# Weight loads in half-transfers of even and odd rows, and a last strip in pieces of 112, 8 and 8 rows, in a decode kernel that streams 89 MB

## The chip, the cores and the metric

The kernel runs on one core of one Trainium2 chip. The time is the device time of one execution in microseconds (us); the lower the better. Before the change it takes 217.38 us, the median of three runs (217.35 to 217.49).

## The reference

Two tokens (B = 2) pass through one decode step of windowed attention, gated by a small MLP:

```python
xn = layernorm(x)                                  # x: (2, 1, 512)
q  = xn @ wq                                       # wq: (512, 4096), 32 heads of 128
k, v = k_cache[:, :, -4096:], v_cache[:, :, -4096:]  # 8 key/value heads, window of 4096
s  = softmax(q k^T / sqrt(128)) v                  # 4 query heads share a key/value head
s  = s.reshape(2, 4096) @ wo                       # wo: (4096, 512)
z  = gelu(xn @ w_in)                               # w_in: (512, 1792)
g  = silu((z1 * (w_sp * layernorm(z2) + b_sp)) @ w_out)   # w_out: (896, 512)
out = x + s * g
```

All of it is in 32-bit floats. Nearly all of the 89.4 MB that are read are the two windows of the caches (32 MiB each) and the weights: w_q 8 MiB, w_o 8 MiB, w_in 3.5 MiB, w_out 1.75 MiB. Each byte is used for two tokens only.

## The kernel before

All large loads go to one ring of four buffers ("slot"), 128 rows of 32 KB each. In order: the two halves of w_q (`wq0`, `wq1`, 32 KB a row), `win` (28 KB a row), `wout` (14 KB a row), then the keys and values of eight units (`k0`, `k1`, `v0`, `k2`, `v1`, ... `v7`, 32 KB a row; a unit is two heads of one token), and last w_o in seven pieces of 8, 8, 8, 4, 2, 1 and 1 blocks of 2 KB a row. A load into a buffer that is still read waits for its readers.

All of these are issued by SP (SyncE), one instruction for each transfer, in the order of the program (the class `InOrder` keeps each engine's instructions in the order in which the code stands; it records every instruction under line 37, so the profile's rows all say L37, and tiles are told by name). ACT (ScalarE) issues three tiny loads at the start: `xs` (two rows of 2 KB) and the two numbers of `wb`. `x`, eight rows of 512 B, is loaded behind the second piece of w_o. A transfer is cut into packets, one for each row here, which 16 DMA engines work off; at the end of its share each of them writes one packet of 4 bytes that counts towards the transfer's completion (the trace has 16 of them for such a transfer). Each transfer has one of eight such counters, named DMAHW0 to DMAHW7 in the lists below; a transfer that takes a counter again waits until the earlier transfer on it is complete.

On the engines: TensorE (PE) makes q from w_q as 128 rows of `wq0` and `wq1` land, then z from `win` and y from `wout`. For a unit VectorE (DVE) transposes the keys in four parts (`kt`), PE makes shares of the scores (`sh`), ACT copies them (`shs`), PE adds them (`s`); then come the maximum, the exponentials (`p`), their transpose (`pT`) and the sum over the values (`acc`). The last w_o blocks go into `part` and `so`; the tail after the last w_o piece is eight small matmuls, two VectorE instructions (`res`) and the store of the output.

Of the kernel before, what the change touches and what calls it, by code (L numbers as in the profile page):

```python
# [14 lines left out]
P = 128  # L15
# [27 lines left out]
def kernel(  # L43
# [14 lines left out]
    pe, dve, act, sp = (InOrder(tc, e) for e in (nc.tensor, nc.vector, nc.scalar, nc.sync))  # L58
# [22 lines left out]
    def slot(name):  # L81
        return ring.tile([P, SLOT], F32, tag="slot", name=name)
# [5 lines left out]
        return ps.tile([P, 512], F32, tag=tag, name=name, bufs=BANKS[tag])  # L88


    xs = cst.tile([B, D], F32, tag="xs", name="xs")
    act.dma_start(xs, x[:, 0, :])
    wq_v = wq.rearrange("(p k) f -> p k f", p=P)
    wqt = []
    for a in range(2):
        t = slot(f"wq{a}")
        sp.dma_start(t, wq_v[:, 2 * a : 2 * a + 2, :].rearrange("p k f -> p (k f)"))
        wqt.append(t.rearrange("p (k f) -> p k f", k=2))
    win = slot("win")[:, : KT * F]
    sp.dma_start(win, w_in.rearrange("(p k) f -> p (k f)", p=P))  # L100
    win = win.rearrange("p (k f) -> p k f", k=KT)
    wout = slot("wout")[:, : FT * D]
    sp.dma_start(wout, w_out.rearrange("(p j) d -> p (j d)", p=P))
    wout = wout.rearrange("p (j d) -> p j d", j=FT)

    wb1 = cst.tile([1, 2], F32, tag="wb1", name="wb1")
# [3 lines left out]
    def by_group(t):  # L110

        return bass.AP(tensor=t.tensor, offset=t.offset, ap=[[DC, G], [D, B], [1, DC]])
# [309 lines left out]
    wo_v = wo.rearrange("(p j) d -> p j d", j=32)  # L422
    blocks = []
    pieces = ((8, 8), (8,), (4, 2, 1, 1))
    j = 0
    for i, piece in enumerate(pieces):
        t = slot(f"wo{i}").rearrange("p (j d) -> p j d", d=D)
        at = 0
        for n in piece:
            sp.dma_start(t[:, at : at + n, :], wo_v[:, j : j + n, :])  # L430
            blocks += [(t, at + a) for a in range(n)]
            at, j = at + n, j + n
            if j == 16:
                sp.dma_start(x4[0:P:16, :], by_group(x))
# [47 lines left out]
    for n in range(EARLY):  # L482
        t, a = blocks[n]
# [5 lines left out]
    for n in range(EARLY, 32):  # L489
        if n == LATE:  # L490
            spread_quarters(so, parts, start=False, stop=False)
        t, a = blocks[n]
# [37 lines left out]
```

## Time and profile before

| what | value | how to read it |
|---|---|---|
| median of three runs | 217.38 us | the time that the change is measured against |
| the profiled execution | 217.5 us, span 215.7 us | the span runs from the first to the last instruction; 1.8 us lie around it |
| PE, DVE, ACT busy | 72%, 50%, 20% of the span | shares of busy time |
| loads on SP's queue (q1) | 96.8% of 16 DMA engines' span | time in packets |
| bytes read from HBM | 89.40 MB, 414 GB/s over the span | |
| instruction loads (q8) and table loads (q14) | 7 packets and 2 | they use the same 16 DMA engines |
| the chain that ended last | DMA 44%, PE 31%, DVE 19% | steps followed back from the last instruction |

A view of the DMA can be asked for a stretch of the span. It counts the packets that *start* in the stretch, their bytes, and their whole time as a share of 16 engines over the stretch. In a short stretch that share can therefore be over 100%, since packets run on past its end; share times length times 16, over the number of packets, is the mean time of a packet.

### The profile page before, as it was taken

How to read it: one execution, taken by the hardware profiler on the slowest of the kernel's cores; microseconds unless marked ns; L12 is line 12 of the kernel's file. 1: busy time of each engine (PE TensorE's matmuls, PEld its weight loads, DVE VectorE, ACT ScalarE, POOL GpSimd, SP SyncE). 2: the span in 40 equal slices, each digit the busy share in tenths (PEclk: the TensorE clock that was granted, in tenths of full speed). 3: DMA queues.
4: the chain of work that ended last, by engine and by line, in shares of the span. 5: the costliest groups of instructions: out<-in, count | busy, mean ns of one | idle time of the engine just before them, and what ended most of it. 6: DMA issues, size and time to landing. Idle time of an engine off the chain costs nothing.

```text
span 215.7 us, 2229 instructions
## 1 busy us (share of the span) xinstructions
PE 155.7 (72%) x866; PEld 43.6 (20%) x866; DVE 108.5 (50%) x176; ACT 44.1 (20%) x109; POOL 2.6 (1%) x14
## 2 busy tenths in 40 slices
PE   0164856151796997899699599459959948998883
PEld 0110212110121222222122222222212212231311
DVE  3400072425976944963946851685577089240101
ACT  5000001401123115114303404120431421242001
POOL 4000000000000000000000000000000000000000
PEclk9999788755589699799889879958988995999699
DMA  7998999999999999999999999999999999999990
GB/s 292 389 486 389 425 433 454 451 416 431 444 395 474 395 459 413 450 425 431 437 400 456 413 444 428 431 437 431 431 407 453 419 444 431 431 401 416 425 377 35
DMA packets 3929, 89.54 MB, mean 415 GB/s; under 512 B 446, under 2 KB 462, under 8 KB 848
## 3 DMA queue, kind: packets, MB, share of 16 engines
q1 hardware_dynamic: 3912, 89.40, 96.8%
q8 instruction: 7, 0.11, 0.2%
q14 instruction: 2, 0.02, 0.0%
q10 hardware_dynamic: 8, 0.00, 0.0%
HBM read 89.40 MB, written 0.00 MB: 414 GB/s over the span
## 4 chain that ended last, share of the span: by engine, by line
DMA 44%; PE 31%; DVE 19%; issue 3%; ACT 1%; SPq 0%; DVEq 0%
DMA k<-in_A_k_cache_dram 22%; DMA win<-in_B_w_in_dram 14%; DVE kt L37 13%; PE s L37 9%; PE sh L37 9%; DMA wo<-in_A_wo_dram 8%; PE acc L37 6%; PE z L37 2%; PE y L37 2%; PE mo L37 1%; DVE gate L37 1%; PE col L37 1%; PE so L37 1%; DVE u L37 1%; DVE m L37 1%
## 5 line engine op out<-in xcount | busy, mean ns | idle before, releaser
L37 DVE STREAM_TRANSPOSE kt<-k 128x2048 f32<-128x2048 f32 x32 | 72.4, 2293 | 24.9 <-DMA k<-in_A_k_cache_dram 24.9
L37 PE MATMUL sh<-kt,qbd 128*32 128x512 f32 x256 | 41.5, 682 | 14.0 <-DVE kt L37 14.0
L37 PE MATMUL s<-shs,add_dq 128*128 128x512 f32 x64 | 41.0, 748 | 0.0
L37 ACT ACTIVATE shs<-sh 128x512 f32<-128x512 f32 x32 | 19.1, 597 | 100.9 <-PE sh L37 100.9
L37 PE MATMUL acc<-v,pT 128*32 128x512 f32 x256 | 32.0, 641 | 0.2 <-DVE pT L37 0.2
L37 PE MATMUL q_ps<-wq,xnT 128*32 128x512 f32 x64 | 11.0, 850 | 9.9 <-DMA wq<-in_A_wq_dram 9.9
L37 PEld LDWEIGHTS s<-shs,add_dq 128*128 128x128 f32 x64 | 11.2, 219 | 28.3 <-issue 23.9
L37 PEld LDWEIGHTS sh<-kt,qbd 128*32 128x32 f32 x256 | 6.9, 115 | 33.9 <-issue 19.6
L37 PEld LDWEIGHTS acc<-v,pT 128*32 128x32 f32 x256 | 7.7, 118 | 25.8 <-issue 23.0
L37 DVE TENSOR_REDUCE m<-s 128x2 f32<-128x512 f32 x8 | 5.4, 680 | 14.0 <-PE s L37 14.0
L37 PE MATMUL mo<-l,same_r 128*128 128x2 f32 x16 | 3.5, 287 | 10.7 <-ACT p L37 10.7
L37 DVE STREAM_TRANSPOSE qT<-q_ps 128x512 f32<-128x512 f32 x2 | 1.4, 717 | 18.1 <-PE q_ps L37 18.1
L37 ACT ACTIVATE o<-acc,wd 128x128 f32<-128x128 f32 x32 | 9.1, 373 | 3.4 <-PE acc L37 3.4
L37 ACT ACTIVATE p<-s,nb 128x256 f32<-128x256 f32 x16 | 7.6, 490 | 7.1 <-DVE nb L37 6.9
L37 PE MATMUL part<-wo,oT 128*32 128x512 f32 x56 | 8.2, 722 | 1.1 <-DMA wo<-in_A_wo_dram 0.8
L37 PE MATMUL col<-o,sel 128*32 128x512 f32 x16 | 8.3, 601 | 0.4 <-ACT o L37 0.4
L37 ACT ACTIVATE zs<-z 128x448 f32<-128x448 f32 x1 | 0.5, 544 | 30.9 <-PE z L37 30.9
L37 PE MATMUL y<-wout,hT 128*32 128x512 f32 x14 | 3.6, 1059 | 3.8 <-issue 3.8
L37 PEld LDWEIGHTS q_ps<-wq,xnT 128*32 128x32 f32 x64 | 2.6, 144 | 17.1 <-issue 12.2
L37 DVE STREAM_TRANSPOSE pT<-p 128x512 f32<-128x512 f32 x8 | 5.4, 675 | 1.2 <-ACT p L37 1.2
L37 DVE TENSOR_TENSOR res<-so,gate 128x128 f32<-128x128 f32 x1 | 0.3, 292 | 11.1 <-PE so L37 11.1
L37 ACT ACT_TABLE_LOAD x4 | 5.1, 1283 | 1.9 <-issue 1.9
(106 smaller groups left out, 66.8 us busy)
## 6 DMA issues: line engine op xcount, KB each, us to landing
k<-in_A_k_cache_dram SPq DMA_DIRECT2D x8, 4096.0 KB, 21.3
v<-in_A_v_cache_dram SPq DMA_DIRECT2D x8, 4096.0 KB, 26.7
wq<-in_A_wq_dram SPq DMA_DIRECT2D x2, 4096.0 KB, 21.3
wo<-in_A_wo_dram SPq DMA_DIRECT2D x3, 2048.0 KB
win<-in_B_w_in_dram SPq DMA_DIRECT2D x1, 3584.0 KB, 29.3
wout<-in_B_w_out_dram SPq DMA_DIRECT2D x1, 1792.0 KB, 33.1
wo<-in_A_wo_dram SPq DMA_DIRECT2D x1, 1024.0 KB
wo<-in_A_wo_dram SPq DMA_DIRECT2D x1, 512.0 KB, 17.4
```

The costliest lines, as they stand in the source:

```text
L37: return self.tc.keep_in_program_order(call(*args, **kwargs))
```

## The change

The kernel's loads of weights are cut otherwise; what is computed, and every instruction of PE, DVE, ACT and GpSimd, stays. `wq0`, `win`, `wout` and the first piece of w_o are each loaded in two transfers of 64 rows, the even rows and then the odd ones. Of `wq1` the first 24 KB of each row come as even and odd rows too; the last 8 KB of each row (2048 numbers) come in three transfers, of rows 0 to 111, 112 to 119 and 120 to 127. All other pieces of w_o, the keys and the values are loaded as before.

```diff
+    def even_odd(dst, src):
+        for r in range(2):
+            sp.dma_start(dst[r:P:2], src[r:P:2])
+
+    def low_heavy(dst, src, n):
+        at = src.shape[1] - n
+        even_odd(dst[:, :at], src[:, :at])
+        for rows in (slice(0, 112), slice(112, 120), slice(120, P)):
+            sp.dma_start(dst[rows, at:], src[rows, at:])
...
         t = slot(f"wq{a}")
-        sp.dma_start(t, wq_v[:, 2 * a : 2 * a + 2, :].rearrange("p k f -> p (k f)"))
+        src = wq_v[:, 2 * a : 2 * a + 2, :].rearrange("p k f -> p (k f)")
+        even_odd(t, src) if a == 0 else low_heavy(t, src, 2048)
...
-    sp.dma_start(win, w_in.rearrange("(p k) f -> p (k f)", p=P))
+    even_odd(win, w_in.rearrange("(p k) f -> p (k f)", p=P))
...
-    sp.dma_start(wout, w_out.rearrange("(p j) d -> p (j d)", p=P))
+    even_odd(wout, w_out.rearrange("(p j) d -> p (j d)", p=P))
...
-            sp.dma_start(t[:, at : at + n, :], wo_v[:, j : j + n, :])
+            if j == 0:
+                even_odd(t[:, at : at + n, :], wo_v[:, j : j + n, :])
+            else:
+                sp.dma_start(t[:, at : at + n, :], wo_v[:, j : j + n, :])
```

The start of SP's program before, from the first load of w_q to the second load of keys (a row has the tile, the source, and rows by numbers a row; `wq_69` and `wq_71` are the two halves, `k_281` and `k_283` the first two units' keys; in brackets is what the instruction waits for):

```order
L37 DMA wq_69<-in_A_wq_dram 128x8192
L37 DMA wq_71<-in_A_wq_dram 128x8192
L37 DMA win<-in_B_w_in_dram 128x7168
L37 DMA wout<-in_B_w_out_dram 128x3584
L37 DMA k_281<-in_A_k_cache_dram 128x1x8192 [waits DMAHW1_49,PE_49]
L37 DMA k_283<-in_A_k_cache_dram 128x1x8192 [waits DMAHW4_49,DMAHW0_49,PE_49]
```

The same place now (`wq_72` is the second half, `k_288` and `k_290` the keys):

```order
L37 DMA wq_69<-in_A_wq_dram 64x8192 x2
L37 DMA wq_72<-in_A_wq_dram 64x6144 x2
L37 DMA wq_72<-in_A_wq_dram 112x2048
L37 DMA wq_72<-in_A_wq_dram 8x2048 [waits DMAHW0_49]
L37 DMA wq_72<-in_A_wq_dram 8x2048 [waits DMAHW1_49]
L37 DMA win<-in_B_w_in_dram 64x7168 [waits DMAHW2_49]
L37 DMA win<-in_B_w_in_dram 64x7168 [waits DMAHW3_49]
L37 DMA wout<-in_B_w_out_dram 64x3584 [waits DMAHW4_49]
L37 DMA wout<-in_B_w_out_dram 64x3584 [waits DMAHW5_49]
L37 DMA k_288<-in_A_k_cache_dram 128x1x8192 [waits DMAHW6_49,PE_49]
L37 DMA k_290<-in_A_k_cache_dram 128x1x8192 [waits DMAHW1_49,DMAHW7_49,DMAHW0_49,PE_49]
```

Four transfers have become eleven, and six of them now wait until a counter of an earlier transfer is free.

The end of SP's program before, from the first piece of w_o to the store:

```order
L37 DMA wo_313<-in_A_wo_dram 128x4096 x2
L37 DMA x_91<-in_A_x_dram 8x1x128
L37 DMA wo_317<-in_A_wo_dram 128x4096
L37 DMA wo_319<-in_A_wo_dram 128x2048
L37 DMA wo_319<-in_A_wo_dram 128x1024
L37 DMA wo_319<-in_A_wo_dram 128x512 x2
L37 DMA out_dram<-res 4x2x128
```

The same place now:

```order
L37 DMA wo_320<-in_A_wo_dram 64x4096 x2
L37 DMA wo_320<-in_A_wo_dram 128x4096
L37 DMA x_98<-in_A_x_dram 8x1x128
L37 DMA wo_325<-in_A_wo_dram 128x4096
L37 DMA wo_327<-in_A_wo_dram 128x2048
L37 DMA wo_327<-in_A_wo_dram 128x1024
L37 DMA wo_327<-in_A_wo_dram 128x512 x2
L37 DMA out_dram<-res 4x2x128
```

Only the first piece has become two; the order is the same.

## The prediction

> **What bounds the kernel now.** I read the page first: the slices of the DMA, its queues, and the chain that ended last.
>
> ```profile
> DMA  7998999999999999999999999999999999999990
> GB/s 292 389 486 389 425 433 454 451 416 431 444 395 474 395 459 413 450 425 431 437 400 456 413 444 428 431 437 431 431 407 453 419 444 431 431 401 416 425 377 35
> q1 hardware_dynamic: 3912, 89.40, 96.8%
> DMA 44%; PE 31%; DVE 19%; issue 3%; ACT 1%; SPq 0%; DVEq 0%
> ```
>
> The DMA engines are busy from the first slice to the last but one, so the 19% of VectorE and 31% of TensorE in the chain run beside transfers. To see whether the engines ever wait for an issue, I asked for the tiles of the keys and of w_o (minimum, median and maximum from issue to landing), and for the end of the chain in order of time.
>
> ```profile
> DMA to landing us min/median/max: 19.0/21.3/23.9
> DMA to landing us min/median/max: 17.4/17.5/17.7
> 193.29 17.36 DMA wo<-in_A_wo_dram
> ...
> 210.70 1.24 PE so L37 x32
> ...
> 211.97 0.47 PE so L37 x8
> ...
> 212.46 0.30 DVE res L37
> ```
>
> A load of keys lands at the earliest 19.0 us after its issue, and its own packets are eight an engine. Next, the DMA in stretches: the middle of the kernel, 13 to 21 us (32 KB packets alone), 31.4 to 34.2 us (14 KB packets alone) and 207 to 212 us.
>
> ```profile
> DMA packets 3261, 85.92 MB, mean 430 GB/s; under 512 B 360, under 2 KB 368, under 8 KB 368
> q1 hardware_dynamic: 3249, 85.81, 99.8%
> q8 instruction: 6, 0.10, 0.2%
> q14 instruction: 2, 0.02, 0.0%
> ...
> q1 hardware_dynamic: 112, 3.67, 106.1%
> ...
> q1 hardware_dynamic: 85, 1.22, 101.5%
> ...
> GB/s 328 393 393 492 426 393 360 426 459 393 328 393 475 361 360 328 459 377 393 426 311 295 213 164 197 180 197 180 180 164 180 115 180 131 115 49 0 0 0 0
> ```
>
> From 4 to 204 us the 16 engines are full (99.8%) at 430 GB/s. A 32 KB packet takes 1.061 x 8 x 16 / 112 = 1.213 us, so a load of keys is 9.7 us of transfer, and its issue is 19.0 - 9.7 = 9.3 us ahead of need at the least. The kernel is bound by its bytes; the time can move only at the start, in the tail, or in how evenly the 16 engines finish. The last row shows that they don't finish evenly: about 209.6 us the rate falls from some 400 to 180 GB/s, half of the engines, for the last 1.7 us. I looked for the reason at one transfer's completions, the second piece of w_o, in four stretches from 199.5 to 200.05, 200.85, 201.25 and 201.6 us, and at one load of instructions (44.2 to 45.3 us).
>
> ```profile
> DMA packets 29, 0.25 MB, mean 451 GB/s; under 512 B 10, under 2 KB 14, under 8 KB 14
> DMA packets 31, 0.38 MB, mean 474 GB/s; under 512 B 4, under 2 KB 8, under 8 KB 8
> DMA packets 9, 0.15 MB, mean 369 GB/s; under 512 B 0, under 2 KB 0, under 8 KB 0
> DMA packets 19, 0.21 MB, mean 609 GB/s; under 512 B 6, under 2 KB 6, under 8 KB 6
> ...
> q8 instruction: 1, 0.02, 6.1%
> ```
>
> Packets under 512 B are completions; those from there to 2 KB are the rows of x, queued right behind. The first stretch has 4 rows of x and 10 completions (two of them x's, so 8 engines finish w_o there); the second again 4 rows of x and 4 completions (two engines); the third none; the fourth six. So eight engines are on time, two are up to 1.3 us late, and six are 1.2 to 2.1 us late. That is the count of the middle stretch: two table loads and six instruction loads, each of which takes time (6.1% of 1.1 x 16 = 1.07 us, and more for what it disturbs) from one engine. The last six set the end. x has eight rows and ran on four engines, two of them on time, the other two the pair that is mildly late; none of the six is among those four.
>
> **The change part by part.** *Shift of bytes.* The strip of 8 KB was 8 rows an engine. If 112 rows go evenly over 16 engines, that is 7 each, and if the two pieces of 8 rows go one row each to the same eight engines, those have 9 and the other eight 7. Price: a 14 KB packet takes 1.015 x 2.8 x 16 / 85 = 0.535 us; with 1.213 us for 32 KB that is 0.0376 us a KB and 0.008 us a packet, so 0.309 us for 8 KB and 0.911 us for 24 KB. Before, wq1 cost an engine 8 x 1.213 = 9.70 us. Now it costs 8 x 0.911 + 7 x 0.309 = 9.45 us, or with 9 strips 10.07: -0.25 us, or +0.37.
>
> *More completions.* Each engine gets one more for wq0, win, wout and the first piece of w_o, and two more for wq1 (four more on the eight that take the small pieces): 6 or 8. No row has one alone; their price lies between nothing and the 0.008 us of a packet. I take the upper end, 0.05 to 0.06 us. So the light engines end 0.20 us earlier and the heavy ones 0.43 us later.
>
> *Who is last.* If the six late engines are light, the fourth stretch above (201.25 to 201.6) moves to 201.05 to 201.4. The pair, if heavy, moves from at most 200.85 to at most 201.28, still not last, and the eight on time stay far ahead. Every later transfer is alike on all engines, so this order holds to the end: -0.20 us. The tail behind the last w_o piece (0.47 + 2 x 0.30 us and the store) stays.
>
> *Even and odd halves.* They move the same bytes. Their price for the rate lies between nothing and a slower rate of the 7 + 3.5 + 1.75 + 2 MiB, of which I know no row; the nearest rows are the full 430 GB/s of all other loads, so I take nothing.
>
> *The start.* Rows from 1.64 to 2.4 us, 2.4 to 2.8 us and 3.5 to 4 us, and the tiny loads of ACT from 1.64 to 1.8 us:
>
> ```profile
> q1 hardware_dynamic: 14, 0.46, 198.7%
> ...
> q1 hardware_dynamic: 2, 0.07, 38.6%
> ...
> q1 hardware_dynamic: 16, 0.52, 243.2%
> ...
> q10 hardware_dynamic: 4, 0.00, 8.4%
> ```
>
> Fourteen engines begin wq0 before 2.4 us and take 1.987 x 0.76 x 16 / 14 = 1.73 us for the first packet; the two that begin later take 0.386 x 0.4 x 16 / 2 = 1.24 us. All 16 begin the second packet between 3.5 and 4 us. So some 0.5 us is lost once. If that comes from handing out 128 rows, 64 rows would halve the late starts: up to -0.5 us. If it is a first read that takes long, nothing changes. Since those that begin first and those that begin last end together, I take the second: 0.
>
> *SP's queue.* Seven more instructions of about 0.4 us at the start (wq's two take 0.86 us) are 2.8 us, and six waits for counters. Behind them stands k0; its cover is the 9.3 us above. Waits at the front are for tiny loads or for parts of w_q, while five transfers issued ahead hold nearly all of w_q, some 19 us of work. I cost them at nothing; with the cover gone each microsecond would count in full. w_o's last pieces, 17.4 us ahead, have the same cover.
>
> The sum against the profiled execution: 217.5 - 0.20 = 217.3 us. It is 0.12 us above the median of 217.38, so against the median 217.2 us.
>
> **Rivals.** *The small pieces queue on each other.* Rows 112 to 119 are next to each other, and eight engines write them at once. For it: two 2 KB rows of xs went side by side to neighbouring partitions, and the q10 row gives 0.084 x 0.16 x 16 = 0.215 us for them and two 4-byte packets; alone they would be 2 x (2 x 0.0376 + 0.008) + 2 x 0.008 = 0.18. Against it: that is only 0.03 us more. If four rows take turns, a piece costs 4 x 0.309 instead of 0.309 us, two pieces 1.85 us more on the heavy engines. The mildly late pair then ends at 200.85 + 0.43 + 1.85 = 203.1, 1.5 us behind the last of now: 218.9 us. It decides from 0.3 us of such waiting, and is measurable from 0.75. The Trainium skill (SBUF — State Buffer, "Door 1: The DMA port swizzle") says just this: a transfer's rate hangs on how many of 16 ports its partitions reach, and partitions 112 to 119 lie on two of them. By it the sum would be 218.9; the xs row speaks rather against so hard a limit.
>
> *The start gains.* 64 rows are handed out in half the time and all engines begin up to 0.5 us earlier: 216.7 to 217.0 us. For it speak the starts spread over 1.64 to 2.8 us.
>
> *The heavy engines are the wrong ones.* x shows only that the six late engines are not among the four that it ran on; four of the first eight stay open. If one of the six is heavy, the end moves by +0.43: 217.8 us. The Trainium skill (DMA: Bandwidth & Descriptors, "Why a DMA increments its semaphore by 16 and not by 1") says that a transfer takes the lowest-numbered engines, as many (up to 16) as divide the slowest dimension of both sides, so eight for these pieces. That x (a source of 4 by 2 rows) ran on four agrees; no view tells engines by number.
>
> *Odd rows cost rate.* If halves with every second row ran 5% slower, 14.25 MiB (14.9 MB at 430 GB/s, 35 us) would cost 1.7 us: 218.9 us. Nothing in this profile tests it.
>
> **How the numbers follow.** A change below 0.2%, 0.43 us, can hardly be told from none here. Shift as planned and no gain at the start: 0.35, 217.2 us (within 0.2%). Start gains too: 0.29, 216.7 to 217.0 (faster). Wrong engines: 0.10, 217.8 (within 0.2%). Small pieces queue: 0.19, 217.9 to 218.9 (slower). Odd rows cost rate: 0.07 (slower). Faster 0.29, same 0.45, slower 0.26. For the range I take 216.65 to 218.4, which leaves out the upper half of the queueing case and most of the last one, about 0.16. The likeliest case's own range is 217.0 to 217.35.
>
> **What would show it.** Right: the fall of the rate before the end is shorter than 1.7 us, the six latest completions of a w_o piece come some 0.2 us earlier against the first eight's 0.4 us later, and 32 KB packets keep 1.213 us. At the start, second packets before 3.5 us mean the start gained. Wrong: strips of 8 KB well over 0.31 us around 20 us, halves of wq0 over 1.213 us a packet, or a gap in the DMA around 20 to 36 us (SP's waits).

## The result, and the profile after

| | before | changed |
|---|---|---|
| median (us) | 217.44 (6 runs, 217.33 to 218.1) | 220.79 (6 runs, 220.65 to 221.15) |
| profiled execution (us), its span | 217.5, 215.7 | 220.71, 218.9 |

The ratio is 1.0152 [1.0138, 1.0167], some 3.3 us slower, and outside the predicted range of 216.65 to 218.4. The page of the changed kernel, with the rows that were read first of before:

```profile
DMA  7999999999999999999999999999999999999990
GB/s 264 407 446 346 306 430 430 431 433 428 431 425 437 425 437 422 443 419 443 425 430 431 431 431 428 431 431 431 431 437 425 446 413 455 407 413 425 423 380 31
q1 hardware_dynamic: 4152, 89.40, 96.7%
DMA 46%; PE 33%; DVE 15%; issue 3%; ACT 1%; SPq 0%; DVEq 0%
```

The engines are as busy as before (96.7% of the span against 96.8%) and move the same 89.40 MB, but in the fourth and fifth slice (16 to 27 us) they move 346 and 306 GB/s, where they moved 389 and 425. So the bytes are late though the DMA engines do not idle. Next the bytes in stretches 0 to 4, 4 to 20, 20 to 28, 28 to 36 and 120 to 204 us, of before:

```profile
DMA packets 36, 1.05 MB, mean 263 GB/s; under 512 B 2, under 2 KB 2, under 8 KB 4
DMA packets 228, 6.82 MB, mean 426 GB/s; under 512 B 20, under 2 KB 20, under 8 KB 20
DMA packets 128, 3.28 MB, mean 410 GB/s; under 512 B 16, under 2 KB 16, under 8 KB 16
DMA packets 221, 3.70 MB, mean 463 GB/s; under 512 B 32, under 2 KB 32, under 8 KB 32
...
DMA packets 1450, 35.98 MB, mean 428 GB/s; under 512 B 164, under 2 KB 172, under 8 KB 172
```

and of the changed kernel, with the share of its engines from 20 to 28 us:

```profile
DMA packets 21, 0.56 MB, mean 140 GB/s; under 512 B 2, under 2 KB 2, under 8 KB 4
DMA packets 312, 6.87 MB, mean 429 GB/s; under 512 B 63, under 2 KB 63, under 8 KB 63
DMA packets 209, 2.52 MB, mean 314 GB/s; under 512 B 37, under 2 KB 37, under 8 KB 37
q1 hardware_dynamic: 209, 2.52, 105.8%
DMA packets 206, 3.34 MB, mean 418 GB/s; under 512 B 47, under 2 KB 47, under 8 KB 47
...
DMA packets 1413, 36.08 MB, mean 430 GB/s; under 512 B 170, under 2 KB 174, under 8 KB 174
```

A packet counts where it begins, so a row is good to about one packet an engine (0.5 MB). By 36 us 14.85 MB had begun before, and 13.29 MB now: 1.56 MB, 3.6 us at 430 GB/s. About half of it (0.76 MB) is missing from 20 to 28 us, at a share of 105.8%. After that the rates are equal (428 and 430 GB/s). The delay arises before 36 us and is carried to the end: the issue-to-landing times of the keys and of w_o, and the end of the chain, are now

```profile
DMA to landing us min/median/max: 20.9/24.7/28.5
DMA to landing us min/median/max: 17.3/17.4/26.8
197.73 17.38 DMA wo<-in_A_wo_dram
...
215.15 0.47 PE so L37 x8
...
215.65 0.30 DVE res L37
```

The last work of TensorE begins at 215.15 instead of 211.97 us, 3.2 us later; what stands behind it is the same. The mean time of a packet shows what is slow (13 to 16 us, 24 KB rows alone; 19.74 to 22.57 us, the strip of 8 KB; 26 to 32 us, win):

```profile
q1 hardware_dynamic: 48, 1.18, 91.2%
...
DMA packets 127, 0.90 MB, mean 318 GB/s; under 512 B 17, under 2 KB 17, under 8 KB 17
q1 hardware_dynamic: 127, 0.90, 102.2%
...
q1 hardware_dynamic: 105, 2.55, 98.9%
```

A 24 KB row takes 0.912 x 3 x 16 / 48 = 0.912 us, as predicted. In the strip 127 - 17 = 110 rows take 1.022 x 2.83 x 16 / 110 = 0.421 us each, where 0.309 was predicted. Over all 128 strip rows the trace has a mean of 0.458 us (up to 1.03), and the 128 rows of win behind them, untouched in size, have 1.235 us (18 of them over 1.2 us, up to 2.84), where before all had 1.062. From 26 to 32 us 105 - 16 = 89 rows of win take 0.989 x 6 x 16 / 89 = 1.067 us: there the old price is back.

### The profile page after: what moved, and what is told of

It is laid out like the page before. It is cut to its first block, busy times and chain, and to the rows that moved or that the text cites. A ratio compares the mean times of both kernels' runs of the same rounds, so it can differ in the third digit from the quotient of the medians.

```text
span 218.9 us, 2242 instructions
## 1 busy us (share of the span) xinstructions
PE 154.8 (71%) x866; PEld 43.7 (20%) x866; DVE 108.5 (50%) x176; ACT 44.0 (20%) x109; POOL 2.6 (1%) x14
## 3 DMA queue, kind: packets, MB, share of 16 engines
q1 hardware_dynamic: 4152, 89.40, 96.7%
HBM read 89.40 MB, written 0.00 MB: 408 GB/s over the span
## 4 chain that ended last, share of the span: by engine, by line
DMA 46%; PE 33%; DVE 15%; issue 3%; ACT 1%; SPq 0%; DVEq 0%
DMA wo<-in_A_wo_dram 20%; DMA win<-in_B_w_in_dram 12%; DMA k<-in_A_k_cache_dram 11%; DVE kt L37 10%; PE s L37 10%; PE sh L37 9%; PE acc L37 7%; DMA wq<-in_A_wq_dram 4%; PE z L37 2%; PE y L37 2%; PE col L37 1%; PE mo L37 1%; DVE gate L37 1%; DVE u L37 1%; DVE m L37 1%
## 5 line engine op out<-in xcount | busy, mean ns | idle before, releaser
L37 PE MATMUL s<-shs,add_dq 128*128 128x512 f32 x64 | 41.5, 756 | 0.0
L37 PE MATMUL q_ps<-wq,xnT 128*32 128x512 f32 x64 | 9.3, 720 | 11.0 <-DMA wq<-in_A_wq_dram 11.0
L37 PE MATMUL z<-win,xnT 128*32 128x448 f32 x32 | 4.6, 735 | 3.8 <-DMA win<-in_B_w_in_dram 3.8
```

The costliest lines, as they stand in the source:

```text
L37: return self.tc.keep_in_program_order(call(*args, **kwargs))
```

## The experiments

Three theories stood at first. The pieces crowd (P in the expectations): the engines that write the strip get into each other's way in SBUF. The halves of every second row cost it, by their rate or their late start (H). SP's queue waits (Q): six issues wait for counters and let the engines run dry. The 105.8% above speaks against Q already. All comparisons are against the kernel before, on the same chip; gains and losses in us are worked out from the ratio.

**The strip alone, the halves alone.** The first leaves everything as before but the strip, the second makes all halves and no strip, the third does without the halves of the first transfer.

```diff
# e1_strip_only, in wq1 (wq0 as before)
+            sp.dma_start(t[:, :6144], src[:, :6144])
+            for rows in (slice(0, 112), slice(112, 120), slice(120, P)):
+                sp.dma_start(t[rows, 6144:], src[rows, 6144:])
# e3_halves_all, against the changed kernel
-        even_odd(t, src) if a == 0 else low_heavy(t, src, 2048)
+        even_odd(t, src)
# e4_halves_later, against e3_halves_all
-        even_odd(t, src)
+        sp.dma_start(t, src) if a == 0 else even_odd(t, src)
```

> Only the strip: wq1 as one transfer of 24 KB a row and then 112, 8 and 8 rows of 8 KB; everything else as before. Theory P (the rows of a small piece lie next to each other, so many engines write into few places and hold each other up): most of the loss comes back, +2.3 to +3.0 us over before, with 8 KB packets well over 0.31 us and long win packets behind them. Theory H (the halves of every second row cost it, by their rate or their late start): within 0.3 us of before. Theory Q (SP's six waits for counters leave the engines idle): about +0.5 us at most, since only the loads of win and wout still wait.

> The changed kernel without the strip: wq1 too is loaded as even and odd rows, whole. Theory P: only what the start loses is left, +0.3 to +0.6 us over before, all of it there when the first half of w_q has landed. Theory H: nearly the whole +3.3 us. Theory Q: part of it, since three waits for counters stay.

> As the run with halves everywhere, but wq0 is one transfer of 128 rows as before, so the very first transfer of the program is the old one. If the loss at the start belongs to the first transfer alone (its issue takes 0.60 us instead of 0.39): within 0.15 us of before. If each pair of halves costs something: +0.1 us for each of four pairs, +0.4 us.

Measured: e1 220.58 against 217.5, 1.0133 [1.0113, 1.0152], +2.9 us. e3 218.2, 1.0028 [1.0017, 1.0039], +0.6. e4 217.7, 1.0009 [0.9999, 1.0019], not told from no change. Here are the DMA rows from 20 to 28 us of e1 and e3, and those from 3.5 to 4 us of the changed kernel (e3 reads the same there) and of e4:

```profile
DMA packets 190, 2.46 MB, mean 308 GB/s; under 512 B 32, under 2 KB 32, under 8 KB 32
```

```profile
DMA packets 149, 3.44 MB, mean 430 GB/s; under 512 B 32, under 2 KB 32, under 8 KB 32
```

```profile
q1 hardware_dynamic: 1, 0.03, 15.3%
```

```profile
q1 hardware_dynamic: 16, 0.52, 246.0%
```

e1 has the slow stretch (308 GB/s) with three transfers at that place and no halves; e3 has as many transfers and waits in SP's queue as the halves make, and runs at 430. The strip is 2.9 us of the loss. What e3 costs lies at the start: all but one of the second packets no longer begin between 3.5 and 4 us, as 16 did before and do in e4. In e3's trace the first 16 packets end 0.46 us later in the mean than before's, and the last packet of w_o still does (211.97 against 211.51 us). SP's issues of w_q (ns, minimum, median, maximum) show part of the reason, before and then changed:

```profile
L37 SPq DMA_DIRECT2D wq<-in_A_wq_dram x2: 386/396/407, 0.7 to 1.2; - x2
```

```profile
L37 SPq DMA_DIRECT2D wq<-in_A_wq_dram x7: 273/590/646, 0.7 to 8.5; - x7
```

The first issue, of 128 rows, took 0.386 us and the first packet began at 1.75 us; of 64 rows it took 0.596 us (0.571 in e3), and the first packet began at 2.11 us (2.08). So the longer issue is some 0.2 of the 0.33 to 0.36 us; where the rest comes from was not shown. 2.9 + 0.6 = 3.5 us against 3.3 measured: the two parts add up within their intervals.

**Where the crowding is.** Four extra transfers of 16 rows by 8 KB into an unused tile go ahead of win, their rows next to each other or seven apart, in SBUF and in DRAM (the four labels). Their bytes alone are 64 x 0.309 / 16 = 1.24 us.

```diff
+    more = cst.tile([P, 2048], F32, tag="more", name="more")
+    more_src = wq_v[:, 3, 2048:4096]
+    for i in range(4):
+        sp.dma_start(more[16*i : 16*i+16], more_src[16*i : 16*i+16])   # adj, adj
# apart: [slice(i, i + 106, 7)] on that side
```

> Before, with four more transfers between wq1 and win: each copies 8 KB of 16 rows of w_q into a tile that nothing reads, here rows 16i to 16i+15 of w_q into rows 16i to 16i+15 of the tile. The bytes alone are 4 x 0.31 = 1.24 us on every engine. Theory P: 16 engines write 16 rows next to each other, four at a time into one place, so +4 us or more in all, with 8 KB packets of 1 us. Theory B (the bytes alone): +1.2 to +1.5 us.

> The same four more transfers, but each takes rows of w_q that are seven apart, and writes them to 16 rows of the tile next to each other. If the crowding is on the side that is written (SBUF): +4 us or more, as with both sides next to each other. If it is on the side that is read (rows near to each other in HBM): +1.2 to +1.5 us.

> The same four more transfers, read from 16 rows of w_q next to each other, and written to rows of the tile that are seven apart. If the crowding is on the side that is written: +1.2 to +1.8 us. If on the side that is read: +4 us or more.

> The same four more transfers, with rows seven apart on both sides. Theory P on either side: +1.2 to +1.8 us, little more than the bytes alone. If small transfers are slow whatever their rows (by their number, or their completions): as slow as the other three.

| SBUF rows | DRAM rows | median of 2 runs (us; before 217.62, 3 runs) | ratio |
|---|---|---|---|
| adjacent | adjacent | 221.9 | 1.0195 [1.0156, 1.0233] |
| adjacent | apart | 221.62 | 1.0182 [1.0145, 1.0218] |
| apart | adjacent | 219.86 | 1.0101 [1.0067, 1.0135] |
| apart | apart | 219.56 | 1.0087 [1.0053, 1.0122] |

The stretch in which nothing but these rows runs, in the same order (2.38, 2.63, 1.58 and 1.50 us long):

```profile
DMA packets 115, 0.47 MB, mean 196 GB/s; under 512 B 58, under 2 KB 58, under 8 KB 58
q1 hardware_dynamic: 115, 0.47, 109.4%
```

```profile
DMA packets 124, 0.51 MB, mean 193 GB/s; under 512 B 62, under 2 KB 62, under 8 KB 62
q1 hardware_dynamic: 124, 0.51, 111.5%
```

```profile
DMA packets 119, 0.48 MB, mean 306 GB/s; under 512 B 60, under 2 KB 60, under 8 KB 60
q1 hardware_dynamic: 119, 0.48, 102.8%
```

```profile
DMA packets 116, 0.48 MB, mean 317 GB/s; under 512 B 58, under 2 KB 58, under 8 KB 58
q1 hardware_dynamic: 116, 0.48, 99.1%
```

One row takes 1.094 x 2.38 x 16 / 57 = 0.73 us, then 0.76, 0.44 and 0.41. What counts is which rows of SBUF are written at once, by a factor of 1.7 to 1.8; the order in DRAM hardly matters. Two expectations were missed: neighbours were to take 1 us a row and took less, and rows seven apart were to cost at most 1.8 us in all and cost 2.2 and 1.9. At 0.41 to 0.44 us they are not undisturbed either; an undisturbed row takes 0.309.

**Halves of neighbouring rows.** wq0 alone as rows 0 to 63 and 64 to 127.

```diff
+            for rows in (slice(0, 64), slice(64, P)):
+                sp.dma_start(t[rows], src[rows])
```

> Before, but wq0 as rows 0 to 63 and then 64 to 127, in place of even and odd rows. If the late start comes from taking every second row: no late start, first packets at 1.75 us. If 64 rows reach only half of the places in SBUF, as theory P and the Trainium skill's port rule (SBUF — State Buffer) have it: the two transfers run at half the rate, 32 KB packets of about 2.4 us, and the kernel is some 9 us slower. If neither: within 0.2 us of before.

Measured 228.38 against 217.5, 1.0493 [1.0476, 1.0511], +10.7 us. From 4 to 12 us:

```profile
DMA packets 56, 1.64 MB, mean 205 GB/s; under 512 B 6, under 2 KB 6, under 8 KB 6
q1 hardware_dynamic: 53, 1.64, 99.8%
```

53 - 3 = 50 rows of 32 KB (three of the queue's packets are completions) take 0.998 x 8 x 16 / 50 = 2.55 us each instead of 1.213: half the rate, with the engines full. Every second row (e3) keeps the full rate, 64 neighbours have half of it. This is the rule of the Trainium skill (SBUF — State Buffer, "Door 1: The DMA port swizzle") that the rate hangs on the number of ports that a transfer's partitions reach; e9 agrees. The first packet is late here too (2.11 us, issue 0.585 us), so that goes with 64 rows and not with every second row.

**Pieces of the strip.** e2 cuts the strip off but writes it whole; e8 has 16 rows in one piece instead of 8 and 8.

```diff
# e2_strip_whole, after the 24 KB of wq1
+            for rows in (slice(0, P),):
# e8_strip_112_16
+            for rows in (slice(0, 112), slice(112, P)):
+                sp.dma_start(t[rows, 6144:], src[rows, 6144:])
```

> The strip kept apart, but not cut by rows: wq1 as 24 KB and then 8 KB of all 128 rows, everything else as before. If the cut by rows makes the loss: within 0.15 us of before. If 8 KB packets or one transfer more cost something by themselves: +0.1 us or more.

> The strip as 112 and 16 rows, so that every engine has 7 + 1 rows and no bytes are shifted; the rest as before. The runs with four extra transfers of 16 neighbouring rows put crowding at about 0.7 us for each. If the 112 rows crowd as well (seven neighbouring rows an engine, so that two engines write to one place at a time): +1.5 to +2.5 us. If only the small pieces crowd: +0.7 us.

e2: 217.8 against 217.48, 1.0016 [1.0006, 1.0026], +0.35 us, more than expected though all its strip rows take 0.309 us in the mean and all rows of win 1.062. e8: 219.59, 1.0097 [1.0084, 1.0111], +2.1 us. From 20 to 28 us e2 and e8 have

```profile
DMA packets 205, 3.51 MB, mean 439 GB/s; under 512 B 16, under 2 KB 16, under 8 KB 16
```

```profile
DMA packets 205, 2.97 MB, mean 372 GB/s; under 512 B 32, under 2 KB 32, under 8 KB 32
```

So cutting by columns is nearly free, and cutting off few neighbouring rows is not. With the pieces of 8 joined most of the loss stays: 112 and 16 rows crowd too.

**The small pieces alone.** The kernel before with two extra pieces of 8 rows by 8 KB into an unused tile, ahead of win; neighbours (e14) or twelve rows apart (e15). Their bytes cost 0.31 us.

```diff
+    for rows in (slice(112, 120), slice(120, P)):          # e14_small_adjacent
+    for rows in (slice(0, 96, 12), slice(1, 97, 12)):      # e15_small_apart
+        sp.dma_start(more[rows], wq_v[rows, 3, 2048:4096])
```

> Before, with the two small pieces alone, as extra work: 8 KB of the rows 112 to 119, and of 120 to 127, copied into a tile that nothing reads, between wq1 and win. That is 2 x 0.31 = 0.62 us more on eight engines, which end early by more than that, so their bytes alone cost 0 to 0.2 us. With crowding: the prediction's rival had four turns for each piece, 1.85 us more on those eight, +1.0 to +1.8 us.

> The same two extra pieces of 8 rows, with rows twelve apart (0, 12, 24 ... 84 and 1, 13 ... 85), which by the port rule of the Trainium skill (SBUF — State Buffer) are all in different places. Theory P: 0 to +0.3 us. If eight rows are slow whatever their distance: as with neighbouring rows.

e14: 219.98 against 217.5, 1.0108 [1.0093, 1.0123], +2.4 us. e15: 218.62, 1.0054 [1.0037, 1.0072], +1.2 us, where hardly any was expected. Both cost more than foreseen. From 20 to 28 us, e14 and e15:

```profile
DMA packets 135, 2.69 MB, mean 336 GB/s; under 512 B 32, under 2 KB 32, under 8 KB 32
```

```profile
DMA packets 152, 3.18 MB, mean 397 GB/s; under 512 B 32, under 2 KB 32, under 8 KB 32
```

In e14 the small rows take 0.66 us in the mean (up to 1.15), and the 128 rows of win 1.231. In e15 the small rows take 0.314 us, so they hardly disturb each other; but of the win rows behind them exactly 16 take 1.32 to 1.50 us instead of 1.062, some 0.34 us more each. That there are 16 small rows too is chance. From 22.73 to 23.14 us all 16 slow rows are in flight at once, so they are the first row of win on each of the 16 engines. It is the same with 128 strip rows (e1: 16 slow rows of win, all in flight at 24.8 us; e8: 16) and with the 64 extra rows above (16, of 1.64 to 2.65 us with neighbours on both sides). In e15, and in e14, eight of them begin by 22.2 us, while the other eight engines are still at their small rows: they run on engines that had none. So small pieces hold up the first row of the next transfer on every engine, and not only on those that wrote a piece. By what path all 16 are held up, when e14's pieces write only 16 neighbouring rows of SBUF, is not shown.

**The shift of bytes without neighbours.** The last KB a row of the last w_o block (late) or of wq1 (early) as 8 groups of 16 rows, meant for eight engines. In e12 and e13 the groups take the rows of DRAM in another order, in which they can't be joined; the last columns then hold other rows, so these two move as many bytes but compute another output.

```diff
+    def eight(dst, src, row, n):
+        ap = [[16 * row, 8], [row, 16], [1, n]]            # e10, e11
+        ap = [[row, 8], [8 * row, 16], [1, n]]             # e12, e13
+        sp.dma_start(dst, bass.AP(tensor=src.tensor, offset=src.offset, ap=ap))
# e10, e12: last block of w_o
+            sp.dma_start(t[:, at, :256], wo_v[:, j, :256])
+            eight(t[:, at, 256:], wo_v[:, j, 256:], 32 * D, 256)
# e11, e13: end of wq1
+            sp.dma_start(t[:, :7936], src[:, :7936])
+            eight(t[:, 7936:], src[:, 7936:], 16384, 256)
```

> Before, with the shift of bytes made where the first eight engines are idle: of the last block of w_o the second half (1 KB of each of the 128 rows) is read as 8 groups of 16 rows, which gives it to eight engines, 16 rows each, in place of 8 rows on each of 16. The late engines have 8 x 1 KB less, about 0.3 us. If engines may write anywhere when they are free: -0.1 to -0.3 us. If writing into the places of the late engines holds those up (theory P): no gain, or +0.1 to +0.5 us.

> The same shift of 1 KB a row by 8 groups of 16 rows, but at the end of wq1, where all engines are full. If bytes can be moved between engines without crowding: -0.2 us, as the prediction had it. If the eight engines crowd (16 packets each, of which several go to one place at once, with the other eight engines in the way): +0.3 to +1.0 us.

> As the run with the second half of the last w_o block in 8 groups of 16 rows, but the groups take every eighth row of w_o, so that they can't be joined to 128 rows (the rows of this half block stand in another order, and the output's last term is another one). Eight completions would show that it ran on eight engines. If the shift of bytes works where the first eight engines are nearly idle: -0.1 to -0.3 us, the late engines ending 0.3 us earlier. If writing into the places of the late engines holds those up: no gain or a loss up to 0.5 us.

> The same at the end of wq1: 1 KB of each row in 8 groups of every eighth row, which can't be joined (the last 256 columns of wq1 hold its rows in another order). If the shift works while all engines are full: -0.2 us. If the eight engines crowd each other and the rest: +0.3 to +1.0 us.

Measured: e10 1.0006 [0.9997, 1.0015], e11 1.0026 [1.0016, 1.0035], e12 1.0022 [1.0012, 1.0031], e13 1.0052 [1.0036, 1.0067], so 0 (not told apart), +0.6, +0.45 and +1.1 us. The first two missed their purpose: the groups were joined to 128 rows again and all 16 engines ran. Over the whole execution the trace has 440 completions on SP's queue before, 456 in e10 and e11, and 448 in e12 and e13: 16 and 8 for the one transfer more. The Trainium skill's rule that the prediction cites (DMA: Bandwidth & Descriptors, "Why a DMA increments its semaphore by 16 and not by 1") agrees with the eight. The end of e12's chain:

```profile
211.08 1.35 PE so L37 x36
...
212.45 0.43 PE so L37 x4
```

e12 takes 8 KB from eight engines and gives it to the other eight, over all 128 rows of SBUF, and still ends 0.45 us later: its last w_o part lands at 212.4 us, before at 211.9. Rows that share the time got longer on both sides: the 1 KB rows of the last block took 0.058 us in the mean (0.047 in e10), the 2 KB rows of the block before it 0.107 (0.085). The relieved engines were mostly the late ones: by the updates of the counters, seven engines ended the first half of the block at 211.77 to 211.98 us, and at most two of them took part in the second half, since six of its eight engines were done by 211.43. So at least five late engines had 8 KB less and ended no earlier than the six late ones before (211.70 to 211.93). In e13 it is alike: 0.054 us for 1 KB rows (0.046 in e11), and win rows of 1.117 us in the mean.

e11's +0.6 us is another matter. Its 1 KB rows take 0.046 us, its rows of win 1.062, and its last packet of w_o ends 0.07 us later than before's. In its profiled run (218.06 us, its median 218.08) the chain ends with 24 matmuls of `part` that take 4.25 us, while TensorE's granted clock is 0.52 of full speed (from 208 to 210 us; before it was 1.00 there). By this trace most of that loss is not in the loads.

## Why the prediction was wrong

*The step that failed: the shift of bytes.* It priced the strip at 0.309 us a row whichever rows run together (-0.25 us light, +0.37 heavy). In the changed kernel the 128 strip rows took 0.458 us in the mean, and those of e1, the strip alone, 0.481. In e1 that is 8 x (0.481 - 0.309) = 1.38 us an engine, and win behind it 8 x (1.233 - 1.062) = 1.37 us more: 2.7 us of its 2.9. e2 and the four x runs show that the rows of SBUF are the cause.

*The right rival, sized too small.* "The small pieces queue on each other" came nearest to the mechanism and had 0.19; it gave 218.9 us. Two things were missing. The piece of 112 rows crowds too (110 rows at 0.421 us; e8, +2.1 us with 16 rows behind it), and the first row of the next transfer, win, is held up on every engine. The rival also let the wait count only where it hit a late engine; in fact fifteen slow rows of win were in flight at once at 25.0 us. Its four turns for a row, 1.24 us, on the other hand, were too many: e14's small rows took 0.66 us in the mean. "The xs row speaks rather against so hard a limit" was the wrong reading: in the traces of other runs, with the same load of xs, the slower of its two rows took from 0.08 us (e1) to 0.94 (e14), so 0.03 us more in one trace said nothing. The rule of the Trainium skill that stood beside it (SBUF — State Buffer, "Door 1: The DMA port swizzle") was on the right side with its 218.9.

*Start: 0.* Wrong, and on the other side of the rival: e3 less e4 is 1.0028 - 1.0009, 0.4 us lost. The first issue, of 64 rows, took longer than one of 128.

*The tail: the shift did what it should, but the order did not hold.* The rate from 210.2 to 215.2 us, and the second piece of w_o from 203.4 to 204.8 and from 204 to 204.4 us:

```profile
GB/s 590 393 295 590 229 393 508 360 573 262 295 410 393 393 393 377 459 361 410 360 311 344 344 246 229 180 344 213 213 197 197 66 66 16 33 0 0 0 0 0
...
DMA packets 49, 0.58 MB, mean 411 GB/s; under 512 B 10, under 2 KB 14, under 8 KB 14
DMA packets 20, 0.18 MB, mean 453 GB/s; under 512 B 7, under 2 KB 9, under 8 KB 9
```

The stretch under 250 GB/s is 1.5 us long, before 1.75 (the 344 in it holds a load of instructions). The 16 updates of the last w_o transfer's counter say more. Before, eight engines ended at 210.1 to 210.3 us, the pair at 210.8 and 211.25, and six at 211.7 to 211.9; now eight end at 212.8 to 213.8 and eight at 214.5 to 215.1. From the median of the first eight to that of the late six it is 1.0 us instead of 1.7 (1.1 in e1; 1.4 to 1.6 in e2, e3, e4 and e8, which shift no bytes). So light and heavy engines drew together by 0.4 to 0.7 us, where 0.63 was planned, which speaks for the late six being light.

But that the pair is "still not last" failed. Before, four rows of x ran on the pair, ahead of the six late completions of w_o. Now two of the four come after 204.4 us, when only three of the completions are left (7 of 10 and 2 of 4 lie before), so an engine of the pair is now among the last to finish that piece; and at the end one engine is 0.3 us behind the other seven that are late. That fits the end which the rival described.

*Right:* the price of 24 KB rows (0.911 against 0.912 us); the halves' rate (28 KB rows of win in e3 at 1.062 us, 32 KB at the old median of 1.215); SP's queue, whose waits cost nothing that can be told from none: the engines were full throughout, and k0's cover of 9.3 us stood. *Odd rows cost rate* got no support, and the tail speaks against *wrong engines*.

*Open:* the 0.35 us of e2, where no packet was slower and the last load landed 0.09 us later; why a first issue of 64 rows takes longer than one of 128; and how the pieces hold up engines that write none of them. The strip's 2.9 us were not split further between 112 rows and the two pieces: e14's +2.4 us for pieces on top of the kernel before and e8's +2.1 overlap.

## What to carry to other kernels

Where the DMA engines are full, cut loads by columns, if at all, and leave all 128 rows in one transfer (e2: +0.35 us); a strip of few rows costs its own packets and those of the transfer behind it. Don't even out engines by giving one engine's rows to another without asking which rows the others write at that time. A full busy share with a fall in GB/s was the sign of the crowding here, and the first transfer of the program was best left the one that is issued fastest. Of the versions tried, none was faster than the kernel before.

## What was not expected of the hardware

- 64 neighbouring rows of SBUF halve the rate of 32 KB packets (2.55 against 1.213 us), every second row doesn't (e9, e3).
- SP took 0.57 to 0.60 us for a first issue of 64 rows and 0.39 us for 128; in e15 the issues of 8 rows, twelve apart, took 0.64 and 0.80 us.
- 16 packets of 8 KB on eight engines, at full speed themselves, made the first 28 KB packet behind them 0.34 us longer on all 16 engines (e15).
